# States copied by chunk for the readout, and another order of the work ahead of the first block

## The chip, the cores and the metric

The kernel runs on one core of a Trainium2 chip. The metric is the device time of one execution in microseconds, the median of several runs.

## What is computed

Three stages follow one another, all in float32 quality:

```python
# 1. linear attention with decay; B, H, S, D = 4, 8, 768, 48
state = alpha[:, :, t, :, None] * state + einsum('bhd,bhe->bhde', k[:, :, t], v[:, :, t])
y[:, :, t] = einsum('bhd,bhde->bhe', q[:, :, t], state)
# 2. a two-layer network on x = y as (3072 tokens, 384)
h = x @ w_in            # 384 -> 2048
x = (h - tanh(h)) @ w_out
# 3. a mixture of 8 experts, one expert a token (argmax of x @ w_gate)
out[mask] = gate_w * eom * (maximum(x[mask] @ w1[e], 0) @ w2[e])
```

## The kernel before

**Units, chunks and states.** The attention is cut into 32 units. A unit is one block of 384 time steps (one batch, one half of the sequence; eight blocks, NBLK) for one pair of heads (four pairs, NP). A unit has six chunks (NC) of 64 steps (CH). The two heads of a pair lie on partitions 0 to 47 and 64 to 111. For each unit these steps follow one another; the letter in brackets is the engine, PE for TensorE, DVE for VectorE, ACT for ScalarE:

- `prep_k` (L173): a backward scan of the decays into Ex and the product kh = k times decay [DVE, two operations].
- `turn_k` (L222): kh is transposed on PE (three matmuls, L226) and copied to ktok by ACT.
- `prep_q1` (L182): a forward scan P of the decays and the reciprocal rP of each chunk's decay [DVE, three operations].
- `decay` (L195): ACT spreads the chunk decays over the tile GE, and sums them into a flag.
- `scale_k` (L198): ACT makes kt = kh times rP, one operation a chunk, six in all; from unit 8 on POOL does it in one.
- `prep_q2` (L206): the product X0 = q times decay [DVE].
- `carry` (L252): clears the incoming state in the PSUM tile pu [DVE], or copies it in from SS of the block before [ACT, L259].
- `update` (L261): the chunks' sums of k times v go into pu [PE, 12 matmuls, L268].
- `chain` (L271): one scan over the chunks turns GE and pu into the states SS, a tile [128, 64, 7] in which the chunk is the last, fastest dimension [DVE, L272].
- `score` (L230): kt against X0, one small matmul a head and chunk [PE, L242, L243].
- `causal` (L245): the scores times a mask, into X1 [DVE, L248].
- `readout` (L285): for each chunk and head one matmul with the state as weights and X0 as moving tile, and one with v (tile WV) as weights and X1 [PE, L306, 24 matmuls, each two records in the trace]; at its end ACT copies the result to y (L309).
- `place` (L311): DVE takes the rest of y that the rounded copy leaves (L315), and the SP queue issues 4 or 6 DMAs that write y into its place in xT, the input of the second stage (L325).
- `alpha_low` (L216): an ACT operation over the raw decays that notes the smallest in a flag.

The states are read for the readout as `SP[rs, :, cc]`, 64 columns at a step of seven elements.

**Who sets the order.** Up to the end of block 0 the order on each engine is the order of the program text (`manual_schedule`); from block 1 on the compiler's scheduler orders all engines but SP, and SP too from block 2, until the last block is in text order again. On an engine an instruction that waits holds all behind it. All DMAs of these stages are issued on SP.

**Ahead of the first block.** L700 to L760 prepare units 0 to 3 (block 0 of the tokens) and begin unit 4: a loop over the units in which unit u is finished (chain, causal, readout) while unit u+1 is prepared (prep_q1, decay, scale_k, carry, update, prep_q2, score) and unit u+2 is begun (`K`, which is prep_k and turn_k). `fill(n)` puts n idle matmuls on PE. Several tiles have one buffer only (kh, kt, P, X1, ktok, the PSUM pair for score and readout), so that each step also waits for the last reader of the unit before.

**Weights.** The second stage's weights come as 64-bit floats and are narrowed to 32 bits by integer operations: `conv(f)` (L359) is six DVE operations (three for the input weight, L336 to L340, three for the output weight WR) with an ACT copy IH (L366) between, and at its end a load of 768 KB (`load_w`, L343) of the weight three steps on. `low_in(f)` (L373) is the DVE operation IL, the rest that IH's rounding leaves.

**The first block.** `first_block` (L762) is called for the 16 values of f. A step does h (PE, nine matmuls with IH and IL, L409), tanh (ACT, L415), a subtraction (DVE, L419), a matmul for the gate (L385, L393), x (PE, L434), and one quarter of the attention work of a unit of the next block, by the phase `ph`: 0 carry, score, update, chain; 1 causal, and prep_k of the next unit; 2 readout and place; 3 turn_k, prep_q1, prep_q2, scale_k. The first two thirds of h for f = 0 are started ahead of the block by `h_begin` (L403). Blocks 1 to 7 do the same in L989 to L1051, with x in three parts.

Of the kernel before, what the change touches and what calls it, by code (L numbers as in the profile page):

```python
# [63 lines left out]
def tile_kernel(ctx, tc, aps, outs):  # L64
# [61 lines left out]
    WV = [ap1.tile([128, WW], F32, name=f"WV{i}") for i in range(2)]  # L126
    GE = [ap1.tile([128, D, NC + 1], F32, name=f"GE{i}") for i in range(2)]
    VZ = [ap1.tile([128, NA, 2, 2 * D], F32, name=f"VZ{i}") for i in range(2)]
    SS = [ap1.tile([128, 64, NC + 1], F32, name=f"SS{i}") for i in range(NP)]

    early = [(psx, "x0"), (psx, "x1"), (psx, "x2"), (psa, "at")] * 4
# [78 lines left out]
    def prep_q(u):  # L210
        yield from prep_q1(u)
        decay(u)
        scale_k(u)
        yield from prep_q2(u)
# [56 lines left out]
    def chain(u):  # L271
        yield dve.tensor_tensor_scan(  # L272
            out=SS[units[u][1]][:, 0:D].rearrange("p d c -> p (d c)"), data0=GE[u % 2].rearrange("p d c -> p (d c)"),
            data1=st[u].pop("pu")[:, 0:(NC + 1) * D], initial=0.0, op0=ALU.mult, op1=ALU.add)

    def weave(*gens):
        gens = [iter(g) for g in gens]
        while gens:
            for g in list(gens):
                if next(g, gens) is gens:  # L280
                    gens.remove(g)
# [3 lines left out]
    def readout(u):  # L285
        j, p = units[u]
        s = st[u]
        ps = s.pop("py") if u >= NP else pair("psy")
        SP, h = SS[p], NC // 2

        for c in range(h):
            for x in range(2):
                for q in range(2):
                    for hh in range(2):
                        cc = q * h + c
                        cs = slice(cc * CH, (cc + 1) * CH)
                        o = ps[64 * q:64 * q + 64, hh, c * CH:(c + 1) * CH]
                        if x == 0:  # L300
                            rs = slice(64 * hh, 64 * hh + D)
                            w, m = SP[rs, :, cc], X0[u % 2][rs, cs]
                        else:
                            rs = slice(64 * hh, 64 * hh + CH)
                            w, m = WV[u % 2][rs, cc * D:cc * D + 64], X1[rs, cs]
                        pe.matmul(o, w, m, start=(c + x == 0), stop=(x == 1), skip_group_check=True)  # L306
        s["y"] = y = (g3.tile([128, 2, TB], F32R, tag="gg", name="y") if 0 < u < 4 else ap1.tile([128, 2, TB], F32R, tag="y", name="y"))
        s["py"] = ps
        act.copy(y[:, 0].rearrange("p (b t) -> p b t", b=2), ps[:, :, 0:TB // 2])  # L309

    def place(u):  # L311
# [365 lines left out]
        pool.memset(WV[i][:, NC * D:WW], 0.0)  # L677
    for p in range(NP):
        pool.memset(SS[p][:, D:64], 0.0)
    warm = psh.tile([128, 512], F32, tag="h", name="warm")  # L680
    junk = ones1[:, 0:192].bitcast(BF16)

# [13 lines left out]
    def K(u):  # L696
        weave(prep_k(u))
        turn_k(u)

    K(0)  # L700
    fill(4)
    weave(prep_q(0))
    carry(0)
    update(0)
    fill(4)
    score(0)
    K(1)
    alpha_low(0)
    load_unit(4)
    for u in range(NP):  # L710
        weave(chain(u))
        if u + 1 < NP:
            weave(prep_q1(u + 1))
            decay(u + 1)
            scale_k(u + 1)
            carry(u + 1)
            fill((0, 2, 2)[u])
            update(u + 1)
            half = [conv_next() for _ in range((0, 0, 1)[u])]
            narrowed(half)  # L720
            weave(prep_q2(u + 1))
            weave(*half)
            for f in list(gw):
                low_in(f)
        if u + 2 < NP:
            K(u + 2)
        if u + 1 < NP:
            score(u + 1)
        weave(causal(u))
        if u > 0:  # L730
            place(u - 1)
        fill((0, 0, 0, 4)[u])
        readout(u)
        if u + 2 < NP:
            load_w_v(u + 2)
        if u + 2 < NP:
            alpha_low(u + 1)
        if u < 2:
            load_v(NP + u)
        if u == 1:  # L740
            load_w(2)
    fill(2)
    half = [conv_next()]
    narrowed(half)
    alpha_low(NP - 1)
    place(NP - 1)
    K(NP)
    fill(4)
    weave(*half)
    gate_turn(0)  # L750
    h_begin(0, 0, range(KC - 1))
    weave(prep_q(NP))
    fill(12)
    alpha_low(NP)
    load_w_v(NP)
    load_w_v(NP + 1)
# [5 lines left out]
    def first_block(f, pend):  # L762
        u, ph = NP + (f + 1) // 4, f % 4
        new = [conv_next()] if nconv < NF else []

        def head():

            gate(f)
            if ph == 0:
                if f:  # L770
                    decay(u)
                carry(u)
                score(u)
                update(u)
            elif ph == 1:
                if u > NP:
                    alpha_low(u)
            elif ph == 2:
                readout(u)
            act.copy(OH[:, f], WR[f])  # L780
            if f + 1 < NF:
                low_in(f + 1)
            for g in new:
                for _ in range(4 if wide else 0):
                    next(g)

        def middle():
            weave(*new)
            if pend and ph != 3:
                x_step(*pend)  # L790
            if ph == 0:
                weave(chain(u))
            elif ph == 1:
                weave(causal(u))
                weave(prep_k(u + 1))
            elif ph == 3:
                x_step(*pend)
                turn_k(u)
                weave(prep_q1(u))
                weave(prep_q2(u))  # L800

        gg = h_step(0, f, (head,))
        middle()
        if f >= NF - 2:
            low_out(f - NF + 2)
        if ph == 0:
            load_v(u + 2)
        elif ph == 1:
            if u > NP:
                load_unit(u + 2)  # L810
        elif ph == 2:
            place(u)
            load_w_v(u + 2)
        if f + 1 < NF:
            gate_turn(f + 1)
        if ph == 3:
            scale_k(u)
        if f == NF - 1:
            decay(u)
            alpha_low(u)  # L820
            load_unit(u + 2)
        return gg

    pend = None
    for j in range(NBLK):
# [163 lines left out]
        for f in range(NF):  # L989
            g = j * NF + f  # L990
            u, ph = 4 + (g + 1) // 4, g % 4
            live = u < len(units)
            if j == 0:
                pend = 0, f, first_block(f, pend)
                continue
            pre = []
            if ph == 1 and live:
                pre.append(chain(u))
                if u + 1 < len(units):
                    pre.append(prep_k(u + 1))  # L1000
            if ph == 2 and u + 1 < len(units):
                pre.append(prep_q(u + 1))
            weave(*pre)
            if j > 0 and f == 2:
                route_score(j - 1)
            if j == 1 and f + 2 < NF:
                low_out(f + 2)
            gg = h_step(j, f)
            if ph == 0 and live:
                score(u)  # L1010
                carry(u)
                update(u)
                if u + 2 < len(units):
                    load_v(u + 2)
                weave(causal(u))
            elif ph == 2 and live:
                readout(u)
                if u + 1 < len(units):
                    alpha_low(u + 1)
                if u + 3 < len(units):  # L1020
                    load_unit(u + 3)
                if u + 2 < len(units):
                    load_w_v(u + 2)
                place(u)
            elif ph == 3 and live:
                turn_k(u)
            if pend is not None:
                x_step(*pend)
                if pend[1] == NF - 1:
                    evac(pend[0])  # L1030
            if j == 1 and f < E:
                sp.dma_start(out=rows[f * NT:f * NT + CAPS[0]].rearrange("(n p) c -> p n c", p=128),
                             in_=blank.unsqueeze(1).to_broadcast([128, CAPS[0] // 128, ROW]))
            if j == 1 and f == 12:
                route_send(0)
            if j > 0 and 2 <= f <= (2 if j == 1 else 3):
                (route_rank, route_send)[f - 2](j - 1)
            pend = (j, f, gg)
            if last:
                if f == 4:  # L1040
                    order()
                    fetch(0, 0)
                    fetch(0, 1)
                if f == 5:
                    gather(0)
                if 8 <= f < 15:
                    split(0, f - 8)
                    if f < 13:
                        fetch(0, f - 6)
                if 10 <= f < 10 + KC:  # L1050
                    turn_x(0, f - 10)  # L1051
# [156 lines left out]
```

## Time and profile before

| | |
|---|---|
| median of 3 runs | 833.27 us (831.03 to 833.64) |
| the profiled execution's own time | 833.43 us |
| its span in the profile | 831.6 us |
| share of the span in which engines are busy | PE 97%, weight loads 90%, DVE 57%, ACT 41%, POOL 16% |
| mean granted TensorE clock | 0.985 of full |
| DMA | 98.53 MB, 118 GB/s over the span |

The span is what the trace covers of one execution. Engines run side by side, so shares don't add up. PE stands for matmuls, PEld for the loads of their weights, which overlap them. A time in brackets at the end of a row of the timeline is how long the engine was idle before it, and who ended that.

### The profile page before, as it was taken

To read this page: it belongs to the slowest core of one execution; us is meant where nothing else is said; L and a number is where in the kernel's file an instruction comes from. 1 tells how busy PE (TensorE), PEld (TensorE's weight loads), DVE (VectorE), ACT (ScalarE), POOL (GpSimd) and SP (SyncE) were. 2 spreads that over 40 slices of the span, in tenths; PEclk is the share of its full clock that TensorE was granted. 3 is DMA by queue.
4 is the path that set the end of the run, shared out by engine and by line. 5 is a ranking of instruction groups with operands and counts; after the bars stand their busy time and mean duration, and the time that the engine had idled before them with its cause. 6 is when DMAs were issued, how large, how long until landed. Compare 5 with 4: busy or idle time off the path is not lost.

```text
span 831.6 us, 16944 instructions
## 1 busy us (share of the span) xinstructions
PE 803.4 (97%) x6688; PEld 745.6 (90%) x6688; DVE 476.7 (57%) x1050; ACT 343.6 (41%) x767; POOL 131.5 (16%) x120
## 2 busy tenths in 40 slices
PE   6699999999999999999999999999999999999995
PEld 4477887999999999999999999999999999999995
DVE  6878888766656665656755753445543434444321
ACT  4445554334434333443433442345443434444421
POOL 1000000020200200200100020021332314424321
PEclk8799999999999999999999999999999999999998
DMA  8465634753323322322332220034525426325400
GB/s 274 145 219 201 209 96 129 241 184 95 97 67 92 95 66 75 111 66 70 88 103 60 71 66 16 15 124 127 176 95 192 151 72 220 136 81 199 158 26 30
DMA packets 64358, 98.53 MB, mean 118 GB/s; under 512 B 20235, under 2 KB 52768, under 8 KB 64272
## 3 DMA queue, kind: packets, MB, share of 16 engines
q1 hardware_dynamic: 60864, 87.91, 34.2%
q0 software_dynamic: 3408, 9.47, 3.0%
q8 instruction: 54, 0.88, 0.4%
q14 instruction: 32, 0.26, 0.1%
HBM read 72.13 MB, written 16.25 MB: 106 GB/s over the span
## 4 chain that ended last, share of the span: by engine, by line
PE 84%; issue 5%; DVE 4%; ACT 3%; DMA 2%; SPq 1%; POOL 1%; POOLq 0%; ACTq 0%; DVEq 0%
PE x L434 26%; PE psh L409 23%; PE o L964 11%; PE psf L936 11%; PE psy L306 4%; PE psu L268 2%; PE psy L242 2%; PE pst L226 1%; PE warm L685 1%; PE pst L915 1%; ACT kt L204 1%; DMA raw<-raw 1%; PE pso L393 1%; DMA s<-w 1%; POOL out L982 1%
## 5 line engine op out<-in xcount | busy, mean ns | idle before, releaser
L409 PE MATMUL psh<-xT,IH 128*128 128x384 f32 x768 | 204.0, 342 | 0.0
L434 PE MATMUL x<-OH,gg 128*128 128x400 f32 x672 | 186.0, 351 | 1.1 <-DVE gg L424 0.5
L409 PEld LDWEIGHTS psh<-xT,IH 128*128 128x128 f32 x768 | 138.3, 189 | 1.0
L409 PE MATMUL psh<-xT,IL 128*128 128x384 f32 x384 | 129.9, 338 | 0.0
L419 DVE TENSOR_TENSOR t<-psh,t 128x384 f32<-128x384 f32 x128 | 70.9, 554 | 97.4 <-ACT t L415 96.8
L434 PEld LDWEIGHTS x<-OH,gg 128*128 128x128 f32 x672 | 121.5, 188 | 5.4 <-DVE gg L424 1.1
L415 ACT ACTIVATE t<-psh 128x384 f32<-128x384 f32 x128 | 62.7, 490 | 130.0 <-PE psh L409 124.5
L434 PE MATMUL x<-OL,gg 128*128 128x400 f32 x336 | 115.9, 345 | 0.0
L964 PE MATMUL o<-hi,hh 128*128 128x384 f32 (+2 forms) x440 | 115.1, 338 | 0.0
L936 PE MATMUL psf<-xe,hi 128*128 128x256 f32 (+6 forms) x432 | 109.3, 338 | 0.0
L942 DVE SCALAR_TENSOR_TENSOR hh<-psf,hh 128x384 fp32r<-128x384 f32 (+3 forms) x96 | 40.9, 447 | 91.8 <-ACT hh L940 90.8
L424 DVE TENSOR_TENSOR gg<-t,gg 128x384 fp32r<-128x384 f32 x112 | 63.6, 568 | 50.1 <-ACT gg L423 47.7
L423 ACT CAST gg<-t 128x384 fp32r<-128x384 f32 x112 | 57.3, 512 | 57.3 <-DVE t L419 56.1
L964 PEld LDWEIGHTS o<-hi,hh 128*128 128x128 f32 (+2 forms) x440 | 78.2, 184 | 1.2 <-DVE hh L942 0.2
L936 PEld LDWEIGHTS psf<-xe,hi 128*128 128x128 f32 x432 | 75.7, 188 | 2.7 <-issue 0.3
L964 PE MATMUL o<-lo,hh 128*128 128x384 f32 (+1 forms) x232 | 77.7, 337 | 0.0
L940 ACT ACTIVATE hh<-psf 128x256 fp32r<-128x256 f32 (+6 forms) x72 | 34.9, 484 | 95.1 <-PE psf L936 75.2
L409 PEld LDWEIGHTS psh<-xT,IL 128*128 128x128 f32 x384 | 72.4, 188 | 0.8
L936 PE MATMUL psf<-xe,lo 128*128 128x256 f32 (+6 forms) x216 | 71.9, 333 | 0.0
L201 POOL TENSOR_TENSOR kt<-kh,rP 128x384 f32<-128x384 f32 x24 | 20.0, 835 | 289.8 <-PE psy L243 166.4
L871 POOL TENSOR_TENSOR lo<-s,hi 128x768 fp32r<-128x768 f32 (+1 forms) x24 | 48.9, 2038 | 94.7 <-ACT hi L870 94.3
L434 PEld LDWEIGHTS x<-OL,gg 128*128 128x128 f32 x336 | 63.2, 188 | 0.0
(146 smaller groups left out, 1151.8 us busy)
## 6 DMA issues: line engine op xcount, KB each, us to landing
raw<-raw SPq DMA_DIRECT2D x32, 579.5 KB
wst<-wio SPq DMA_DIRECT2D x16, 768.0 KB
s<-w SPq DMA_DIRECT2D x24, 512.0 KB
s<-w SPq DMA_DIRECT2D x32, 384.0 KB
xT<-y SPq DMA_DIRECT2D x96, 72.0 KB
rows<-blank SPq DMA_DIRECT2D x8, 772.0 KB
WV<-vw SPq DMA_DIRECT2D x32, 144.0 KB
VZ<-vn SPq DMA_DIRECT2D x60, 72.0 KB
```

What stands on the lines that cost most here:

```text
L306: pe.matmul(o, w, m, start=(c + x == 0), stop=(x == 1), skip_group_check=True)
L409: pe.matmul(begun[f][:, 0:TB], w[:, f, c], xT[j][:, x, kc], start=(kc + n == 0), stop=(kc == KC - 1 and n == 2))
L415: act.activation(out=t, in_=ps[:, 0:TB], func=AF.Tanh)
L419: dve.tensor_tensor(out=g, in0=ps[:, 0:TB], in1=t, op=ALU.subtract)
L423: act.copy(gg[:, 0], g)
L424: dve.tensor_tensor(out=gg[:, 1], in0=g, in1=gg[:, 0].bitcast(F32), op=ALU.subtract)
L434: pe.matmul(px[j][a][:, 0:DG], g, w, start=(f == 0 and n == 0), stop=(f == NF - 1 and n == len(parts) - 1))
L871: (dve, pool)[i % 2].tensor_tensor(out=lo, in0=t, in1=hi.bitcast(F32), op=ALU.subtract)
L936: pe.matmul(ps[:, 0:n], w[:, kc, fs], xe[:, x, kc], start=(i == 0), stop=(i == 3 * KC - 1))
L940: act.activation(out=hh[:, 0:n], in_=ps[:, 0:n], func=AF.Relu)
L942: dve.scalar_tensor_tensor(out=hh[:, o:o + c.stop - c.start], in0=ps[:, c], scalar=0.0, in1=hh[:, c].bitcast(F32), op0=ALU.max, op1=ALU.su ...
L964: pe.matmul(po[q][m][0:p.stop - p.start, 0:DM], hh[:, p], w[:, f], start=(f == 0 and i == 0), stop=(f == NFE - 1 and i == len(parts) - 1))
```

## The change

Three things change. First, a tile SC [128, 6, 64] holds the states by chunk: `by_chunk` has ACT copy SS into it in phase 1 of each unit from unit 4 on, and `readout` takes its weights from it there, 64 columns side by side. Units 0 to 3 still read SS. Second, the work ahead of the first block is put in another order: scale_k ahead of decay, the ACT copy y taken out of readout (`y_copy`) and put behind the next unit's scale_k and decay, alpha_low behind these too, the narrowing of the first weight behind readout(2) and score(3), that of the second in two halves around place(3), K(4) and prep_q1(4), gate_turn(0) ahead of K(4), low_in(1) ahead of the block, and six fills where there were twelve. Third, in the first block decay stands behind update, and for f = 0 chain stands ahead of the rest of conv.

```diff
+    SC = ap1.tile([128, NC, 64], F32, name="SC")
...
+    def by_chunk(u):
+        act.copy(SC[:, :, 0:D].rearrange("p c d -> p d c"), SS[units[u][1]][:, 0:D, 0:NC])
...
-                            w, m = SP[rs, :, cc], X0[u % 2][rs, cs]
+                            w, m = SP[rs, :, cc] if u < NP else SC[rs, cc], X0[u % 2][rs, cs]
...
+        s["py"] = ps
+        if u >= NP:
+            y_copy(u)
+
+    def y_copy(u):
+        s = st[u]
+        ps = s["py"]
         s["y"] = y = ...
-        s["py"] = ps
         act.copy(y[:, 0].rearrange("p (b t) -> p b t", b=2), ps[:, :, 0:TB // 2])
...
+    pool.memset(SC[:, :, D:64], 0.0)
...
     K(0)
     fill(4)
-    weave(prep_q(0))
+    weave(prep_q1(0))
+    scale_k(0)
+    decay(0)
+    weave(prep_q2(0))
     carry(0)
     update(0)
     fill(4)
     score(0)
     K(1)
-    alpha_low(0)
     load_unit(4)
     for u in range(NP):
         weave(chain(u))
         if u + 1 < NP:
             weave(prep_q1(u + 1))
+            scale_k(u + 1)
             decay(u + 1)
-            scale_k(u + 1)
+        if u > 0:
+            y_copy(u - 1)
+        alpha_low(u)
+        if u + 1 < NP:
             carry(u + 1)
             fill((0, 2, 2)[u])
             update(u + 1)
-            half = [conv_next() for _ in range((0, 0, 1)[u])]
-            narrowed(half)
+        if u == NP - 2:
+            weave(causal(u))
+            place(u - 1)
             weave(prep_q2(u + 1))
-            weave(*half)
-            for f in list(gw):
-                low_in(f)
-        if u + 2 < NP:
-            K(u + 2)
-        if u + 1 < NP:
+            readout(u)
             score(u + 1)
-        weave(causal(u))
-        if u > 0:
-            place(u - 1)
-        fill((0, 0, 0, 4)[u])
-        readout(u)
+            half = conv_next()
+            narrowed([half])
+            weave(half)
+            low_in(0)
+        else:
+            if u + 2 < NP:
+                weave(prep_k(u + 2), prep_q2(u + 1))
+                turn_k(u + 2)
+                score(u + 1)
+            weave(causal(u))
+            if u > 0:
+                place(u - 1)
+            fill(4 if u == NP - 1 else 0)
+            readout(u)
         if u + 2 < NP:
             load_w_v(u + 2)
-        if u + 2 < NP:
-            alpha_low(u + 1)
...
-    fill(2)
-    half = [conv_next()]
-    narrowed(half)
-    alpha_low(NP - 1)
+    half = conv_next()
+    for _ in range(3 if wide else 0):
+        next(half)
+    y_copy(NP - 1)
     place(NP - 1)
+    gate_turn(0)
     K(NP)
-    fill(4)
-    weave(*half)
-    gate_turn(0)
+    weave(prep_q1(NP))
+    weave(half)
+    low_in(1)
+    scale_k(NP)
+    weave(prep_q2(NP))
+    decay(NP)
     h_begin(0, 0, range(KC - 1))
-    weave(prep_q(NP))
-    fill(12)
+    fill(6)
     alpha_low(NP)
...
             if ph == 0:
-                if f:
-                    decay(u)
                 carry(u)
                 score(u)
                 update(u)
+                if f:
+                    decay(u)
...
             act.copy(OH[:, f], WR[f])
-            if f + 1 < NF:
+            if ph == 1:
+                by_chunk(u)
+            if 0 < f < NF - 1:
                 low_in(f + 1)
...
         def middle():
+            if f == 0:
+                weave(chain(u))
             weave(*new)
...
             if ph == 0:
-                weave(chain(u))
+                if f:
+                    weave(chain(u))
...
             weave(*pre)
+            if ph == 1 and live:
+                by_chunk(u)
```

## Rows read from the trace of the kernel before

**Rows 1.** The page, part 1: busy time, share of the span and instructions of each engine
```profile
PE 803.4 (97%) x6688; PEld 745.6 (90%) x6688; DVE 476.7 (57%) x1050; ACT 343.6 (41%) x767; POOL 131.5 (16%) x120
```
**Rows 2.** Stages: us; busy of PE, PEld, DVE, ACT, POOL; granted clock; DMA share, GB/s
```profile
20.00:30.00 10.00, 6.11 (x102) 4.39 (x101) 7.69 (x16) 6.94 (x24) 0.00 (x0) 0.76 0.31 76
...
38.50:45.30 6.80, 6.01 (x21) 4.36 (x22) 4.71 (x13) 3.58 (x12) 0.00 (x0) 0.50 0.31 83
...
130.00:590.00 460.00, 458.64 (x4241) 434.11 (x4239) 282.48 (x658) 187.10 (x431) 53.20 (x54) 1.00 0.32 93
```
**Rows 3.** Timeline of PE in readout(4): start us, us, what, xcount
```profile
57.55 0.46 PE L306 MATMUL psy<-X,SS 48*64 48x64 f32 x8
57.83 0.29 PE L306 MATMUL psy<-X,WV 64*64 64x64 f32 x8
57.95 0.41 PE L306 MATMUL psy<-X,SS 48*64 48x64 f32 x8
58.19 0.29 PE L306 MATMUL psy<-X,WV 64*64 64x64 f32 x8
```
**Rows 4.** Instructions of L306 and L242: ns min/median/max, first and last start us, forms
```profile
L306 PEld LDWEIGHTS psy<-X,SS x768: 187/208/228, 17.9 to 520.2; 48*64 48x64 f32 x192
...
L242 PEld LDWEIGHTS psy<-X,kt x336: 129/135/135, 47.7 to 514.1; 48*64 48x64 f32 x168
```
**Rows 5.** Timelines of DVE, ACT and PE around one unit of block 2
```profile
207.29 0.84 DVE L272 TENSOR_TENSOR_SCAN SS<-GE,psu 128x336 f32<-128x336 f32 x1
...
208.17 0.73 ACT L196 ACTIVATE GE<-P 128x288 f32<-128x288 f32 x1 [2.02 <-DVE SS L272]
...
210.79 0.46 PE L306 MATMUL psy<-X,SS 48*64 48x64 f32 x8
```
**Rows 6.** Timeline of ACT ahead of the first block, units 0 and 2
```profile
19.65 0.48 ACT L309 CAST y<-psy 128x384 fp32r<-128x384 f32 x1 [2.28 <-PE psy L306]
...
21.33 1.52 ACT L204 ACTIVATE kt<-kh,rP 128x64 f32<-128x64 f32 x6
```
**Rows 7.** Timeline of DVE ahead of the first block
```profile
18.18 0.19 DVE L192 RECIPROCAL rP<-rP 128x6 f32<-128x6 f32 x1
...
22.89 0.56 DVE L180 TENSOR_TENSOR kh<-raw,Ex 128x384 f32<-128x384 f32 x1 [2.01 <-ACT kt L204]
...
26.41 0.39 DVE L336 TENSOR_SCALAR w<-wst 128x384 int32<-128x384 int32 x1
...
29.35 0.55 DVE L208 TENSOR_TENSOR X<-raw,P 128x384 f32<-128x384 f32 x1
...
30.98 0.55 DVE L315 TENSOR_TENSOR y<-psy,y 128x384 fp32r<-128x384 f32 x1
...
33.83 0.56 DVE L315 TENSOR_TENSOR y<-psy,y 128x384 fp32r<-128x384 f32 x1
...
37.21 0.55 DVE L315 TENSOR_TENSOR y<-psy,y 128x384 fp32r<-128x384 f32 x1
```
**Rows 8.** SP queue ahead of the first block: its timeline, and its waits
```profile
31.59 12.33 SPq L325 DMA_DIRECT2D xT<-y  x16
...
SPq L325 <- DMA wst<-wio: 1.9, 1, 1.9
```
**Rows 9.** Timeline of PE around the start of the first block
```profile
39.29 0.90 PE L226 MATMUL pst<-cst,kh 128*128 128x128 f32 x3 [2.93 <-DVE kh L180]
...
41.77 0.99 PE L409 MATMUL psh<-xT,IH 128*128 128x384 f32 x2
...
43.84 2.87 PE L685 MATMUL warm<-ones,oneb 128*128 128x384 bf16 x12
46.41 0.65 PE L409 MATMUL psh<-xT,IH 128*128 128x384 f32 x2
...
50.33 0.55 PE L385 MATMUL pso<-cst,WR 128*128 128x128 f32 x3 [1.02 <-DVE SS L272]
```
**Rows 10.** Timeline of PE in the first block, update of unit 5
```profile
69.64 0.72 PE L268 MATMUL psu<-VZ,ktok 128*64 128x96 f32 x12 [0.33 <-ACT psu L259]
```

## The prediction

> **What bounds the kernel now.** I read the page first: TensorE (PE) is busy 97% of the span, VectorE (DVE) 57%, ScalarE (ACT) 41% [rows 1]. Then the table by stage: in the 460 us from 130 us on PE lacks 1.4 us; in the ten from 20 us it lacks 3.9, at a mean clock of 0.76 [rows 2]. So there are two regimes. In the long one a microsecond is won only by taking work off PE. Ahead of the first block PE waits, and what counts there is a chain over ACT, DVE and the SP queue that ends in the block's input xT. The timelines of the three engines show that chain: ACT stands 2.28 us behind a readout before it may go on to the next unit [rows 6], DVE stands 2.01 us for ACT's kt before kh [rows 7], and PE fills with idle matmuls until xT is there [rows 9].
>
> The change touches both. All sums are against the profiled execution, 833.43 us, whose span is 831.6; the median of the runs, 833.27, lies 0.16 below it, so the two can be read as one.
>
> **Part 1, the readout.** A readout is 48 matmul records in six groups of eight. A group on SS takes 0.28 and 0.24 us from start to start, a group on WV 0.12 [rows 3]. The form table of the two lines says why: weights from SS load in 208 ns (median), weights from kt in 135, though both have 48 rows and 64 columns and stand beside the same moving tile X0 [rows 4]. SS is read with a step of seven elements, kt side by side; that is what differs. SC lies side by side, so an SS group should take the time of a WV group: 3 x (0.24 - 0.12) = 0.36 us a unit. Bounds: nothing, if something other than the loads spaces the groups, and 0.36. I take 0.33, near the WV group, which stands in the same stream; a tenth is kept back because a WV group now has slow groups beside it and will then share its pace with fast ones. Units 4 to 31 are 28: **28 x 0.33 = 9.2 us** (0 to 10.1), all of it on PE's path by rows 2.
>
> The Trainium skill speaks against this part: "TensorE: Matmul & The Clock Gate", section LDWEIGHTS, gives a load's time as its columns over 1.2 GHz, whatever the pattern it reads, which makes an estimate of 53 ns for both tiles. By it the copy would buy nothing and the sum would lose 9.2 us; the trace does not agree, with 208 against 135 ns for the same 64 columns.
>
> **Its price.** by_chunk adds 28 ACT copies of 128x288, strided on both sides; no row has that form. From below: a copy of 384 elements side by side takes 0.48 [rows 6], so 288 some 0.4. From above: GE, 288 elements in a strided pattern, takes 0.73 [rows 5]. I take 0.6, 17 us of ACT in all. What hides it: in the unit shown the scan that makes SS ends at 208.13 and its readout starts at 210.79 [rows 5], so the copy fits between, and ACT is four tenths busy. Queued behind it on ACT is the next tanh, for which DVE and then PE's x matmuls wait. I charge 0.7 us over the whole run, 0 to 2. Without the cover each copy would cost its 0.6, 17 us. POOL's memset of SC's border runs while nobody waits for POOL: nothing.
>
> **Part 2, the work ahead of the first block.** I walk down the queues with the rows' durations.
> Unit 2 is the large step. rP(2) is ready at 18.37 [rows 7], yet kt(2) starts at 21.33, because ACT has y(0), held by the readout until 19.65, and then alpha_low and GE ahead of it [rows 6]. With scale_k first and y_copy and alpha_low behind, kt(2) follows rP(2), itself some 0.8 earlier since kt(0) and kt(1) no longer stand behind a GE of 0.7. So kt(2) runs from 17.6 to 19.1, and kh(3) moves from 22.89 to 19.1.
> From kh(3) to the first narrowing operation DVE has 3.52 us of work (22.89 to 26.41) [rows 7]. The same operations, with a short wait for y(0), bring rP(3) at 22.8; kt(3) 1.52 and GE 0.7 on ACT, then y(1) 0.48, give place(1) at 25.5 (before 30.98).
> Now DVE runs without a wait: place, X0, IL and causal at 0.5 each, six narrowing operations 2.94 (26.41 to 29.35), chain 0.84 [rows 5, 7]: place(2) at 31.3, before 33.83. The narrowing is not saved, only moved behind readout(2) and in front of chain(3).
> place(2) 0.5, readout(3) 1.2 at full clock and y(3) 0.48 give place(3) at 33.7, before 37.21; three narrowing operations lie under that readout.
> On SP, ten xT issues stand behind place(2). Before, sixteen took 12.33 us, 1.9 of it waiting for a wst load to land, so 0.65 each [rows 8]; ten from 31.8 end at 38.3. One wst load goes ahead of place(1)'s six issues and one behind them, no longer both ahead. The landing of the last has no row: it lies 0 to 2.5 us after the issue's end at 43.92, since the third part of h starts at 46.41 [rows 8, 9]. I take 1.4, the middle: 39.7. A walk of the same kind down the kernel before ends 0.4 early, so 40.1.
> PE: K(4)'s transposes start 2.08 us after place(3), as before (37.21 to 39.29) [rows 7, 9], and take about 0.7, so h's first two parts, which need xT of units 0 to 2 alone, start at 36.5; they took 2.07 (41.77 to 43.84), and the fill behind them is now 6 matmuls, not the 12 that took 2.57 with the clock low for most of them [rows 9]. Six at that low clock take up to 1.9: the third part of h at 40.4 in place of 46.41, 6.0 us.
> The clock gives some back. Before, it was 0.50, the level of 1.2 GHz, from 38.5 to 45.3, PE having stood idle for 2.93 us until 39.29; in the long regime it is 1.00, the level of 2.4 GHz [rows 2, 9]. After, PE pauses until about 36, so the third part of h, gate and score may run at 1.2 GHz; at 2.4 they took some 2 us, so 0 to 1.5 is lost; I take 0.5. **Part 2 gains 5.5 us**, 3.5 to 7.
>
> **Part 3, the first block.** PE waits 1.02 us for chain(4) [rows 9]; that scan was already next when its update ended, so putting it ahead of two narrowing operations gives nothing, 0 to 0.3, and low_in(1) moves to where DVE waits for h. Decay behind update takes 0.7 us of GE off ACT ahead of the copy into psu, for which PE waits 0.33 us [rows 10]; that pattern stands three times (units 5, 6 and 7): 1.0 us, 0 to 1.
>
> **Sum:** 9.2 + 5.5 + 1.0 - 0.7 = 15.0, and 833.4 - 15.0 = **818.4 us**. Bounds, the zero of part 1 being rival A: 7.0 + 3.5 + 0 - 2 = 8.5 and 10.1 + 7 + 1 = 18.1, so 815.3 to 824.9.
>
> **Rivals.** A: the loads are not what spaces the groups, and part 1 gives 0: 833.4 - 5.8 = 827.6. For it, the fast pace of WV is only ever seen with SS groups between; against it, rows 4. Chance 0.08. This is the case that the rule of the Trainium skill describes ("TensorE: Matmul & The Clock Gate", LDWEIGHTS).
> B: the early order gives nothing, because the wst load of 768 KB that now lies between the xT pieces holds the SP queue as it did for 1.9 us before and the pieces land behind it, or because the half clock lasts into the block: 833.4 - 9.5 = 823.9. Against it, one such load is then in flight at a time. Chance 0.07.
> C, slower: from block 1 on the compiler's scheduler orders ACT, and already there ACT idles 2.02 us behind the scan with a GE and a tanh queued [rows 5]. If by_chunk is queued so in front of the tanh, each tanh is late by the copy and a wait. It decides once 0.65 us of that reaches PE in each of the 24 units of blocks 1 to 6, which eats up the 15.7 of gain; at 0.9 us it is 21.6 and 833.4 - 15.7 + 21.6 = 839.3. Against it, PE lacks 1.4 us in 460 with such a wait already there. Chance 0.04.
> The forecast has 0.78; 0.03 is left for a better order than mine.
>
> **Numbers.** The range 814 to 826 takes in the bounds of the sum, B, and a microsecond beyond either; A and C, 0.12, lie outside. About 0.3%, 2.5 us, is what a measurement of this kernel can tell from no change. Faster 0.93: the forecast, B, the better order, and A but for 0.03, where a poor part 2 goes with it and the time is the same, 0.03; slower 0.04, C.
>
> **What would show it.** SC's groups 0.12 us apart and its loads at 135 to 150 ns; kh(3) near 19 and the third part of h near 40; the three waits of 0.33 us gone; copies of 0.4 to 0.7 us. It is wrong if SC's groups stay at 0.24, if PE waits in front of x matmuls for ACT, or if the last xT issue still starts after 41.

## The result, and the profile after

The changed kernel takes **820.82 us** (median of 4 executions, 819.37 to 824.24) where the kernel before, beside it, takes 832.49 (831.03 to 833.64): a ratio of 0.9867, 95% interval 0.9831 to 0.9902, so 11.7 us were won where 15.0 had been forecast. The profiled execution of after is the slowest of its four: its own time is 824.24, its span 822.4. So single spans are read below with a second profiled execution of the same kernel beside them (span 819.2).

Part 1 of the page, after, answers to [rows 1]. ACT has 28 instructions more, the copies, which take 20 us; its busy time rose by 14.6 us. PE's fell by 10.6 us.

```profile
PE 792.8 (96%) x6676; PEld 736.8 (90%) x6676; DVE 473.9 (58%) x1050; ACT 358.2 (44%) x795; POOL 131.5 (16%) x121
```

**The readout.** Timeline of PE in readout(4) of after, to be held against [rows 3]: start us, us, what, count. SC groups and WV groups now follow one another every 0.12 us, the first 0.16. The last line is PE's next operation: the readout is over after 0.86 us.

```profile
55.68 0.34 PE L311 MATMUL psy<-X,SC 48*64 48x64 f32 x8
55.84 0.30 PE L311 MATMUL psy<-X,WV 64*64 64x64 f32 x8
55.96 0.30 PE L311 MATMUL psy<-X,SC 48*64 48x64 f32 x8
56.08 0.30 PE L311 MATMUL psy<-X,WV 64*64 64x64 f32 x8
...
56.54 2.28 PE L445 MATMUL x<-WR,t 128*128 128x400 f32 x6
```

The same next operation before, 1.21 us behind the first line of [rows 3]:

```profile
58.76 0.94 PE L434 MATMUL x<-WR,t 128*128 128x400 f32 x2
```

The loads of that line and of the score, and the copy, after (count; ns min/median/max; first and last start us; forms), against [rows 4]. SC loads in 133 ns; SS, still read by units 0 to 3, in 210 ns.

```profile
L311 PEld LDWEIGHTS psy<-X,SC x672: 129/133/134, 55.7 to 511.6; 48*64 48x64 f32 x168
...
L311 PEld LDWEIGHTS psy<-X,SS x96: 187/210/223, 15.9 to 32.4; 48*64 48x64 f32 x96
...
L244 PEld LDWEIGHTS psy<-X,kt x336: 129/135/227, 43.2 to 505.6; 48*64 48x64 f32 x168
...
L279 ACT COPY SC<-SS x28: 703/713/722, 51.8 to 507.4; 128x288 f32<-128x288 f32 x28
```

**The work ahead of the first block.** Timeline of DVE, after, against [rows 7]: kh(3), and place of units 1, 2 and 3.

```profile
18.94 0.56 DVE L182 TENSOR_TENSOR kh<-raw,Ex 128x384 f32<-128x384 f32 x1 [0.34 <-ACT kt L206]
...
25.32 0.56 DVE L326 TENSOR_TENSOR y<-psy,y 128x384 fp32r<-128x384 f32 x1 [2.16 <-ACT y L320]
...
30.86 0.55 DVE L326 TENSOR_TENSOR y<-psy,y 128x384 fp32r<-128x384 f32 x1
...
33.41 0.56 DVE L326 TENSOR_TENSOR y<-psy,y 128x384 fp32r<-128x384 f32 x1 [0.55 <-ACT y L320]
```

Timeline of the SP queue, after, against [rows 8]: the last ten xT issues.

```profile
31.92 7.19 SPq L336 DMA_DIRECT2D xT<-y  x10
```

Timeline of PE, after, against [rows 9]: K(4)'s transposes, the third part of h for f = 0, the first transposes of the weights for the gate behind chain(4). The starts are earlier by 3.4 to 5.6 us, but the two h matmuls take 0.98 us, as those at 41.77 in [rows 9] that ran at 1.2 GHz; before, the two that begin the third part took 0.65.

```profile
35.49 0.90 PE L228 MATMUL pst<-cst,kh 128*128 128x128 f32 x3 [2.17 <-DVE kh L182]
...
40.85 0.98 PE L420 MATMUL psh<-xT,IH 128*128 128x384 f32 x2
...
46.90 0.90 PE L396 MATMUL pso<-cst,WR 128*128 128x128 f32 x3 [1.03 <-DVE SS L274]
```

The table by stage, after (us; busy of PE, PEld, DVE, ACT, POOL; granted clock; DMA share, GB/s), shows the clock there: between 33.3 and 50.2 us it stands at 0.50, 16.9 us long, while around the start of the block it was low before from 38.5 to 45.3 [rows 2]. And from 130 to 590 us PE now lacks 4.5 us where it lacked 1.4 (0.9 of it are two waits of the next stage, which begins earlier and now lies inside).

```profile
33.30:50.20 16.90, 13.14 (x73) 10.86 (x73) 11.95 (x26) 6.43 (x20) 0.00 (x0) 0.50 0.65 209
...
130.00:590.00 460.00, 455.51 (x4274) 431.09 (x4273) 278.52 (x661) 199.67 (x456) 55.13 (x54) 1.00 0.33 97
```

The tanh steps show what the low clock took. Timeline of ACT, before: first and second tanh.

```profile
47.27 0.49 ACT L415 ACTIVATE t<-psh 128x384 f32<-128x384 f32 x1 [1.86 <-PE psh L409]
52.50 0.49 ACT L415 ACTIVATE t<-psh 128x384 f32<-128x384 f32 x1 [1.11 <-PE psh L409]
```

The same of after: the first is 5.1 us earlier, the second only 1.9.

```profile
42.19 0.49 ACT L426 ACTIVATE t<-psh 128x384 f32<-128x384 f32 x1 [2.13 <-PE psh L420]
50.60 0.49 ACT L426 ACTIVATE t<-psh 128x384 f32<-128x384 f32 x1 [2.28 <-PE psh L420]
```

**The long regime.** PE's waits from 60 to 565 us (line waited at, released by: us in total, times, longest), before. In these lists t and gg are the tiles between tanh and x, and lz the gate's results, which DVE copies out of a finished block's x.

```profile
PE psu L268 <- ACT psu L259: 1.0, 3, 0.3
PE x L434 <- DVE gg L424: 0.5, 1, 0.5
PE x L434 <- DVE lz L471: 0.4, 1, 0.4
PE psy L306 <- issue: 0.3, 1, 0.3
```

and after:

```profile
PE psh L420 <- DMA xT<-y: 0.9, 1, 0.9
PE psy L244 <- ACT ktok L230: 0.7, 1, 0.7
PE psh L420 <- issue: 0.7, 1, 0.7
PE psh L420 <- DVE t L430: 0.6, 1, 0.6
PE x L445 <- DVE lz L482: 0.4, 1, 0.4
```

The three waits of [rows 10] are gone. In their place stand a wait of the score for ktok and one of h for xT, both where block 2 begins, and one of h where block 7 begins ("issue" says that the profile shows nothing that it waited for). The wait for t, at 166 us, stands about where x waited for gg before. Timeline of PE, after, where block 2 begins:

```profile
197.76 0.29 PE L244 MATMUL psy<-X,kt 48*64 48x64 f32 x2 [0.72 <-ACT ktok L230]
198.99 0.58 PE L420 MATMUL psh<-xT,IH 128*128 128x384 f32 x2 [0.94 <-DMA xT<-y]
...
200.51 1.23 PE L270 MATMUL psu<-VZ,ktok 128*64 128x96 f32 x12
```

Behind them the clock falls for a moment: the update takes 1.23 us, as at 1.2 GHz, where it takes 0.72 in [rows 10].

### The profile page after: what moved, and what is told of

It is laid out like the page before. It is cut to its first block, busy times and chain, and to the rows that moved or that the text cites. A ratio compares the mean times of both kernels' runs of the same rounds, so it can differ in the third digit from the quotient of the medians.

```text
span 822.4 us, 16944 instructions
## 1 busy us (share of the span) xinstructions
PE 792.8 (96%) x6676; PEld 736.8 (90%) x6676; DVE 473.9 (58%) x1050; ACT 358.2 (44%) x795; POOL 131.5 (16%) x121
## 4 chain that ended last, share of the span: by engine, by line
PE 83%; DVE 5%; issue 5%; DMA 3%; ACT 2%; SPq 1%; POOL 1%; POOLq 0%; DVEq 0%; ACTq 0%
PE x L445 25%; PE psh L420 24%; PE o L993 11%; PE psf L965 11%; PE psy L311 3%; PE psy L244 3%; PE psu L270 2%; DMA raw<-raw 1%; PE pso L404 1%; PE pst L944 1%; PE pst L228 1%; DMA s<-w 1%; DVE P L190 1%; DMA xT<-y 1%; ACT kt L206 1%
```

## Experiments

Theory 1: two losses hide in the result. The low clock ahead of the block and in its first step eats part of the early order's gain; and reading SC makes the scheduler put PE's work of block 1 in another order, which leaves PE without work where block 2 begins. Theory 2: both are chance of the one profiled execution. Theory 3, which came up later: the copies themselves hold up ACT. None of the kernels leaves out a part of the computation. All ratios are to the kernel before on the same chip, whose median was 832.0 us beside the first four, 832.2 beside the next four and 833.0 beside the last four.

**again: the changed kernel as it is.**

> The changed kernel once more, to see what of its trace stands and what belongs to one execution. Theory 1 (two losses against the sum: the clock stays at half from about 33 to 50 us because PE pauses ahead of the first block, some 3 us; and the scheduler's other order from block 1 on lets PE wait and lose the clock where block 2 begins, some 3 us): both are seen again, the second tanh of the first block near 50.6 and PE idle again near 198; the time is 820 to 824. Theory 2 (the losses are chance of that execution): the clock is back by 44 us, the second tanh comes near 47.5, no wait near 198, and the time is 816 to 819.

Measured: 821.71 us, ratio 0.9874 (0.9858 to 0.9890). The two waits at block 2 are there again (0.72 and 0.93), and so is that at block 7; the wait for t, at 163 us here, was 0.9. They belong to the kernel, which speaks against theory 2. The clock is not the same: it was low from 32.5 to 42.6 only, the second tanh stood at 48.40, and it did not fall at block 2. How long the low clock lasts thus changes with the execution, and in this theory 2 was right.

**sc_only: part 1 alone on the kernel before.**

```diff
+    SC = ap1.tile([128, NC, 64], F32, name="SC")
...
+    def by_chunk(u):
+        act.copy(SC[:, :, 0:D].rearrange("p c d -> p d c"), SS[units[u][1]][:, 0:D, 0:NC])
...
-                            w, m = SP[rs, :, cc], X0[u % 2][rs, cs]
+                            w, m = SP[rs, :, cc] if u < NP else SC[rs, cc], X0[u % 2][rs, cs]
...
+            if ph == 1:
+                by_chunk(u)
...
```

> The kernel before with part 1 alone: the copies by chunk and the readout from them. Both theories expect readouts of 0.86 us in place of 1.21, 28 of them, 9.8 us of PE work. Theory 1: the scheduler's order from block 1 on is disturbed as in the changed kernel and gives some 3 to 4 back, so 6 faster than before, 826 to 827. Theory 2: nothing is given back, 9 to 10 faster, 823.

Measured: 825.89 us, 0.9931 (0.9914 to 0.9947): 6.1 us for part 1. PE's waits from 60 to 565 us:

```profile
PE psu L269 <- ACT psu L260: 1.0, 3, 0.3
PE psh L413 <- DMA xT<-y: 0.9, 1, 0.9
PE psy L243 <- ACT ktok L229: 0.7, 1, 0.7
PE psh L413 <- DVE t L423: 0.7, 1, 0.7
PE psh L413 <- issue: 0.7, 1, 0.7
PE x L438 <- DVE lz L475: 0.4, 1, 0.4
```

The new waits come with part 1, whatever stands ahead of the first block: 1.6 us at block 2 and 0.7 at block 7. The three of 0.33 stay without part 3.

**order_only: parts 2 and 3 alone.**

```diff
...
-                            w, m = SP[rs, :, cc] if u < NP else SC[rs, cc], X0[u % 2][rs, cs]
+                            w, m = SP[rs, :, cc], X0[u % 2][rs, cs]
...
-            if ph == 1:
-                by_chunk(u)
...
```

> The changed kernel without part 1: no copies, the readout from SS. Theory 1: the order alone gives about 2 us ahead of the second tanh, because the half clock takes the rest, and 1.0 from the three waits of 0.33 us in the first block: 829 to 830.5. Theory 2: 5.5 and 1.0, 826 to 827. If the boundary of block 2 shows the same wait here, the copies are not its cause.

Measured: 826.73 us, 0.9942 (0.9920 to 0.9964): 5.3 us. In its profiled execution the clock is low from 34.0 to 40.7 only, and the second tanh stands at 46.90, 5.6 us earlier than before. PE's waits from 60 to 565 us are two:

```profile
PE x L441 <- DVE gg L431: 0.5, 1, 0.5
PE x L441 <- DVE lz L478: 0.4, 1, 0.4
```

So nothing is lost at block 2 while the readout reads SS. Its six executions run from 825.26 to 830.74 us, the fastest at a mean clock over the span of 0.989, the slowest at 0.978.

**more_fill: the changed kernel with more idle matmuls,** so that PE pauses less ahead of the block and in its first step.

```diff
         if u == NP - 2:
+            fill(8)
...
-            fill(4 if u == NP - 1 else 0)
+            fill(12 if u == NP - 1 else 0)
...
     gate_turn(0)
+    fill(12)
...
                 if f:
                     decay(u)
+                else:
+                    fill(5)
```

The first of these lines stands behind the update of unit 3.

> The changed kernel with idle matmuls put into PE's four pauses: 8 ahead of readout(2), 12 in place of 4 ahead of readout(3), 12 behind gate_turn(0), 5 behind the first update of the block. Theory 1: the clock is at full from about 40 us, the second tanh comes near 47.5 in place of 50.6, and the kernel is 2.5 to 3.5 faster than the changed one, 817 to 818. Rival: fills at half clock stand in the way of readouts and transposes, the third part of h comes later than 41 and nothing or less than 1 us is won.

Measured: 821.59 us, 0.9876 (0.9861 to 0.9892), no better than the changed kernel. In its profiled execution the early part is cured: the clock stands at 1.00 from 6.6 to 197.6 us and the second tanh at 46.73. But the start that was won arrives at block 2 as a longer wait for xT, and there the clock falls to 0.50. Timeline of PE:

```profile
195.71 0.59 PE L420 MATMUL psh<-xT,IH 128*128 128x384 f32 x2 [1.30 <-DMA xT<-y]
...
197.24 0.88 PE L270 MATMUL psu<-VZ,ktok 128*64 128x96 f32 x12
198.05 1.01 PE L420 MATMUL psh<-xT,IH 128*128 128x384 f32 x2
```

So the next step is to take the two losses away together.

**copies_unread: the copies are made, and every readout reads SS.**

```diff
-                            w, m = SP[rs, :, cc] if u < NP else SC[rs, cc], X0[u % 2][rs, cs]
+                            w, m = SP[rs, :, cc], X0[u % 2][rs, cs]
```

> The new early order and the 28 copies into SC, but every readout reads SS, so the copies serve nobody; TensorE's instructions stand in the order of the kernel with the new early order alone (826.73 us). Theory 1, the copies cost next to nothing and the loss in the blocks comes from TensorE's other order: 826.7 to 827.4 us, no new TensorE wait where block 2 begins. Theory 3, the copies on ACT themselves hold the tanh and cost 0.1 us each: 829.5 us, and TensorE waits in front of x matmuls for DVE or ACT in many steps.

Measured: 826.45 us, 0.9941 (0.9920 to 0.9963), as order_only. PE's waits from 60 to 565 us:

```profile
PE x L445 <- DVE gg L435: 0.6, 1, 0.6
PE x L445 <- DVE lz L482: 0.4, 1, 0.4
```

28 copies of 0.71 us, 20 us of ACT, cost nothing that can be seen: theory 3 is out. PE's operations follow one another in this trace, from 60 us to the end of block 6, as in that of order_only, while the changed kernel has another order in blocks 1 to 6. So it is the reading of SC that makes the scheduler choose that order, not the copies. Whether the scheduler moves work because it takes the readout for shorter, or because the readout now stands behind one more operation, no run here tells.

The order can be counted in the traces. From the update of unit 8 on, readout(11) stands behind 117 matmul records of h in order_only and copies_unread, and behind 126 in the repeated run; one h has nine. With it the xT pieces of unit 11, which the third part of the first h of block 2 needs, come one h later against PE's other work. From readout(11) to the update of unit 12, PE has 27 records of h in order_only, and 15 in the repeated run.

**unit8: the changed kernel, with unit 8 alone on SS.** With that, the scheduler gives block 1, from unit 10 on, the order that the later blocks have anyway.

```diff
-                            w, m = SP[rs, :, cc] if u < NP else SC[rs, cc], X0[u % 2][rs, cs]
+                            w, m = SP[rs, :, cc] if u < NP or u in (8,) else SC[rs, cc], X0[u % 2][rs, cs]
...
-            if ph == 1 and live:
+            if ph == 1 and live and u not in (8,):
                 by_chunk(u)
```

> The changed kernel, but the readout of unit 8 alone still reads SS and has no copy; units 4 to 7 and 9 to 31 read SC. With it, TensorE's order through block 1 settles in the pattern that the later blocks have anyway. Theory 1: the waits where block 2 begins (0.72 and 0.93 us in the repeated run) and the excess of 0.3 us at 163 us go, one readout gives back 0.36: 821.7 - 1.95 + 0.36 = 820.1 us. Theory 3 (what is lost in the blocks is the copies' doing, whatever the order): the waits turn up elsewhere and only the 0.36 is seen: 822.0 us.

Measured: 820.65 us, 0.9857 (0.9836 to 0.9878). PE's waits from 60 to 565 us:

```profile
PE x L445 <- DVE gg L435: 1.0, 1, 1.0
PE psh L420 <- issue: 0.7, 1, 0.7
PE x L445 <- DVE lz L482: 0.4, 1, 0.4
```

Both waits at block 2 are gone, and readout(11) stands behind 117 records of h again. The wait at 163 us, which I had expected to shrink, stayed (1.0 for x, where h waited 0.9). Against the repeated run the profiled execution is 1.3 us ahead at the second tanh (47.09 against 48.40) and 3.3 us at the end (815.9 against 819.2): 2.0 us came in the blocks, more than the 1.65 - 0.36 = 1.3 of the sum; where the rest comes from is open. The medians do not show it: the intervals of this run and of the repeated one overlap, and the five executions run from 817.2 to 822.0, at mean clocks between 0.989 and 0.979. That the waits go is shown; what it gains in time is seen in one execution.

**unit8_fill: unit8 and more_fill together.**

> As the run with unit 8 on SS, and the added idle matmuls ahead of the first block and in its first step that held the granted clock at 1.00 from 6.5 us on. Theory 1 (two losses, half clock and order, that add): second tanh at 46.7 in place of 48.4, no half clock and no wait of over 0.4 us where block 2 begins: 820.1 - 1.6 = 818.5 us. Rival, that TensorE's waits there are set by the xT transfers and only move with the start: the h matmuls of block 2 wait again, over 0.7 us, and the time is 819.8 to 820.5 us.

Measured: **817.67 us**, 0.9823 (0.9810 to 0.9836), better than both kernels; the five executions lie between 816.55 and 818.74, at clocks from 0.992 to 0.996. By the ratios, against the repeated run, more_fill alone gained nothing, unit8 alone 1.4 us, within the noise, and both together 4.2. There are two losses, as theory 1 has it, and they hide one another. Even here the profiled execution met a low clock, from 42.8 to 46.2, behind a wait of 1.34 us for xT. A stage within it:

```profile
42.90:46.10 3.20, 3.20 (x27) 2.09 (x25) 1.45 (x3) 0.75 (x2) 0.00 (x0) 0.50 0.96 314
```

**unit8_fill_x: on top of it, in the first step of block 7, x before the third part of h.**

```diff
+            if last and f == 0:
+                h_begin(j, f, range(KC - 1))
+                x_step(*pend)
             gg = h_step(j, f)
...
-                x_step(*pend)
+                if not (last and f == 0):
+                    x_step(*pend)
```

> As the run before it, and in the first step of block 7, which runs in the written order, the first two parts of h and the last x step of block 6 go ahead of the third part of h, which waits 0.71 us for xT at 513.4 us in the repeated run. Theory 1: that wait goes: 818.5 - 0.7 = 817.8 us. Rival: the tanh of that step, 1.6 us later, is then late for x, TensorE waits there instead, and nothing is won: 818.5 us.

Measured: 817.99 us, 0.9826 (0.9813 to 0.9839): nothing won, as the rival had it. The wait of 0.7 us in front of the third part of h goes, and one of 0.9 for lz comes in front of the next x, at 514.6 us. In this execution the clock stayed up in the first block and PE came to 162 us earlier; there its wait for gg was 1.6 us in place of 1.0.

**decay_first: unit8_fill with decay of units 5 to 7 ahead of update again.** The other half of part 3, chain ahead of the rest of conv for f = 0, stays.

```diff
+                if f:
+                    decay(u)
                 carry(u)
                 score(u)
                 update(u)
-                if f:
-                    decay(u)
```

> On top of the kernel with unit 8 on SS and the added fills (817.67 us): part 3 undone, GE of units 5 to 7 goes ahead of the copy into psu again. Theory (part 3 is worth the three waits of some 0.33 us): TensorE waits 0.33 us for that copy three times, 818.7 us. Rival (the waits were covered by something else, or GE then holds up another ACT step instead): 817.7 us.

Measured: 819.38 us, 0.9845 (0.9832 to 0.9858). The three waits are back in the list of waits:

```profile
PE psu L270 <- ACT psu L261: 1.0, 3, 0.3
```

By the ratios that is 0.0022, or 1.8 us, little more than the noise (the two intervals overlap by a little); the profile accounts for 1.0 of it.

**decay_scale: unit8_fill with GE ahead of kt again in the early part.**

```diff
...
+            decay(u + 1)
             scale_k(u + 1)
-            decay(u + 1)
```

> On the same base: ahead of the first block, GE of each unit goes before its kt again, as before the change; the rest of the new early order stays. Theory (the chain over ACT and DVE sets the end of the early work, as the walk had it): kt one GE of 0.7 later for units 0 to 2, kh(3) 1.4 to 2.1 later than 19, the last xT and the second tanh as much later: 819.1 to 819.8 us. Rival (the SP queue with the xT pieces sets it already): kh(3) is late but the last xT issue is at most 0.5 later, 818.0 us.

Measured: 819.32 us, 0.9838 (0.9825 to 0.9851), 1.2 us by the ratios: between the two, and within the noise. kh(3) starts at 20.12 in place of 19.04, less late than I had it; place(2) at 31.43 in place of 30.98; the last xT issue ends at 40.16 in place of 39.21. So DVE makes up for part of the delay in the waits that it has anyway, and the SP queue does not: the pieces of place(0) start at 21.78 in place of 20.70, those of place(1) at 27.92 in place of 26.84, and the last ten at 32.67 in place of 31.80. place(2) ends at 31.98 here, 0.7 ahead of its pieces; what holds these is the queue, with the wst load ahead of them. The chain over ACT and DVE sets when the queue begins, and the queue hands the delay on.

**late_w3: unit8_fill with the fourth weight load behind the xT pieces.**

```diff
-        if f + STG < NF:
+        if 0 < f < NF - STG:
             load_w(f + STG)
...
     place(NP - 1)
+    load_w(STG)
```

> On the same base: the load of the fourth weight block (768 KB), which stands on the SP queue ahead of the xT pieces of units 2 and 3, goes behind them. Theory (SP queue and transfers set the end): the last xT piece lands 1.0 us earlier than 40.8, the wait of h for it (1.34 and 0.64 us in two executions of that early part) shrinks by as much, 816.8 us. Rival (the pieces are ready no earlier): nothing moves, 817.7 us; or the narrowing of that block then waits for its load, 818.5 us.

Measured: 820.37 us, 0.9855 (0.9838 to 0.9873), so slower. The last piece and with it the first tanh were earlier, 41.09 in place of 41.76. Now PE has its waiting for xT in one piece, where unit8_fill waited 1.2 and 1.3 us, and the table by stage shows what follows it. PE's waits from 33 to 50 us:

```profile
PE psh L420 <- DMA xT<-y: 2.3, 1, 2.3
```

The stage from 41.4 us:

```profile
41.40:48.10 6.70, 6.70 (x52) 5.55 (x52) 4.02 (x8) 1.95 (x6) 0.00 (x0) 0.50 1.07 410
```

PE is busy without a gap here, at 1.2 GHz, and the second tanh stands at 49.06. Whether the wait brought the low clock, and whether the other executions lost their time in the same way, is open; the mean clocks of the four, 0.988 to 0.993, are below those of unit8_fill by little.

**late_w2: unit8_fill with the third weight load behind the pieces.**

```diff
-        if u == 1:
-            load_w(2)
...
     place(NP - 1)
+    load_w(2)
```

> On the same base: the load of the third weight block, which stands ahead of the xT pieces of unit 1, goes behind all pieces, while the fourth stays where it is. Theory: the pieces of units 1 and 2 land earlier, but that load, some 5 us long, then comes when the first block wants it: DVE waits for it, and the second or third tanh is 1 to 2 us later: 818.7 us. Rival: it has the slack, and the last piece lands up to 1 us earlier: 816.8 us.

Measured: 821.71 us, 0.9866 (0.9852 to 0.9880). That load is wanted at once: DVE's queue stands 3.8 us for it, chain(4) behind it, and PE waits 2.6 us for chain(4). Of the places tried, those of the change are the best.

## Why the prediction was right, and where it was not

**Part 1, the loads.** Right. From its first matmul to PE's next operation a readout takes 0.86 us (55.68 to 56.54 in readout(4) of after) in place of 1.21; three groups are faster by 0.12 each, 0.36 in all, where 0.33 had been taken: 28 x 0.36 = 10.1 us of PE's work, the upper bound of that term. PE's busy time fell by 10.6, but fewer idle matmuls and another clock are in that number too. The tenth held back for mixed pace was not needed: WV groups stay at 0.12 beside fast ones. Rival A falls. The rule of the Trainium skill behind it ("TensorE: Matmul & The Clock Gate", LDWEIGHTS: a load's time goes by its columns; a step between the elements read is not named there) does not hold here: 210 ns from SS against 133 from SC, for the same 64 columns, and neither is near the 53 that was estimated from it.

**The price of part 1** is the term that failed. It charged 0.7 us for ACT copies in front of tanh. The copies are longer than the estimate (0.71, not 0.6) and cost nothing that can be seen (copies_unread). What does cost is the scheduler. The prediction had its freedom in view, in rival C, but for ACT. It was PE's order that it changed: unit 11's readout now comes one h later against the work around it, and where block 2 begins too little is left to do while xT is on its way. sc_only won 6.1 us (4.4 to 7.2 by its interval) where 9.2 - 0.7 = 8.5 had been forecast; PE's waits from 60 to 565 us rose from 2.2 to 4.4, and unit8 shows the cause of the two at block 2 by taking them away. The 0.7 at block 7 stays in every kernel that reads SC but unit8_fill_x, where another wait takes its place. "All of it on PE's path by rows 2" was true; that PE's path would stay as full was taken for granted.

**Part 2, the walk.** Right to half a microsecond, but for the SP queue: kh(3) 18.94 for 19.1, place(1) 25.32 for 25.5, place(2) 30.86 for 31.3, place(3) 33.41 for 33.7, the last xT issue's end 39.11 for 38.3, the third part of h 40.85 for 40.4. The SP queue was 0.8 late: place(2)'s pieces began at 31.92 and took 0.72 each, not 0.65, and 0.7 us of its waiting was for the wst load that rival B named. The load held the queue, but by less than a microsecond.

**The clock** is the other term that was mis-sized. It was charged with 0.5, 0 to 1.5. In the profiled execution of after it took 5.1 - 1.9 = 3.2 us, since it stayed low through the update, the wait for chain(4) and the second h, until 50.2. Five profiled executions have this early part unchanged, and the second tanh stands in them ahead of that of before by 1.9 us (after), 4.1 (again), 5.4 (copies_unread and unit8) and 5.6 (order_only). So 5.5 is what part 2 gives when the clock rises by 41 us. The foot of these differences is not firm either: sc_only has the early part of before, and its second tanh stands at 51.61, not 52.50. By the median order_only has 5.3 for parts 2 and 3, where 6.5 had been forecast, but 6.5 lies within its interval (3.0 to 6.7). Rival B's second half, a low clock that lasts into the block, happens in some executions. The cure (more idle matmuls, with the block 2 waits gone) is worth 3.0 us between the medians of unit8 and unit8_fill.

**Part 3.** Right: the wait of 1.02 us for chain(4) stays (1.03), the three of 0.33 are gone, and putting decay back ahead of update costs 1.0 in waits (decay_first).

**The sum.** 15.0 forecast, 11.7 measured. By the medians of the parts alone: 2.4 are missing in part 1 (8.5 to 6.1) and 1.2 in parts 2 and 3 (6.5 to 5.3), together 3.6 for the 3.3. Only the first of the two is clear of the noise. In the lower bound of the sum, the 7.0 for part 1 is worked out from no row; the result does not hang on it.

## What to carry to other kernels

Where a scheduler orders an engine that is full, count a saving on it only after comparing its instruction order before and after: a step that was only meant to become shorter can move work away from the place where it covered a transfer, and one step left in the old form may restore it. Where work ahead of a full stretch is pulled forward, what the engine loses at the lower clock is a term of its own, here up to 3.2 us where the walk itself was right to half a microsecond; look at several executions, and try idle work in the pauses. Two such losses can hide one another, so a cure that shows nothing alone should be tried together with the other.

## What had not been expected of the hardware

The same program meets the lower clock in one execution and not in another. unit8_fill and unit8_fill_x are the same up to block 7: in one the clock was low from 42.8 to 46.2 us, behind waits for xT of up to 1.3 us, in the other it stayed at 1.00, behind waits of up to 1.1. The stage of the latter:

```profile
18.30:800.00 781.70, 772.38 (x6533) 719.51 (x6527) 456.41 (x1012) 346.19 (x765) 125.51 (x103) 1.00 0.38 118
```

decay_first waited 1.9 and 0.6 us there and stayed at 1.00; late_w3 waited 2.3 us in one piece and then ran 6.7 us at 1.2 GHz without a gap. In these runs, then, a pause of one to two microseconds was a risk and not a fixed price. The five times of unit8 spread by 4.8 us, the five of unit8_fill, which has the idle matmuls, by 2.2.
